# 128-column weight loads, and value mixing of two batches at a time from a channel-major copy, in an attention and SwiGLU kernel

## The chip, the core and the metric

The kernel runs on one core of a Trainium2 chip. Times are device microseconds of one execution. Ratios are always taken between fast runs of the same call on the same chip, because the median of the kernel before moved between 309.9 and 312.1 us from call to call. A run more than 1.5% above the fastest of its kernel counts as slow and is left out of the ratios.

The engines are named as the profile names them: PE is TensorE (matmuls), PEld its weight loads, DVE VectorE, ACT ScalarE, POOL GpSimd. An eviction copies a result from a PSUM tile, where the kernel's matmuls put it, to SBUF. The head is the first part of a run, until the attention of batch 0 is done (about 52 us in the kernel before).

## The reference, cut to what matters

Batch 4, 8 heads, 768 positions, head width 64, 8 blocks of 96 positions. A Sinkhorn iteration makes an 8 x 8 mixing matrix P for each head. Keys and values are mixed block by block with P, then attention runs inside each block, and a SwiGLU feed-forward follows over all 3072 tokens.

```python
k_sorted = einsum('bhij,bhjcd->bhicd', P, k_b)
v_sorted = einsum('bhij,bhjcd->bhicd', P, v_b)
scores = scale * matmul(q_b, k_sorted^T)          # 96 x 96 in each block
attn = exp(scores) / sum(exp(scores))
x = matmul(attn, v_sorted)                        # 96 x 64 in each block
out = (silu(x @ w_gate) * (x @ w_val)) @ w_out    # 512 -> 1536 -> 512
```

## The kernel before

A batch has 64 rows of (head, block); two batches share one SBUF tile of values. The parts that the change touches:

```python
# values of one batch: 64 partitions, [96 positions (padded to 128), 64 channels]
v_tiles[b] = vnp.tile([128, 128, D], BF16, ...)       # odd b uses the tile of b - 1

def drain(dst, src):          # evictions from PSUM: DVE and ACT by turns
    ...

def emit_v(b):                # value mixing: 64 matmuls for a batch
    for db in range(D // 8):
        tp = psum.tile([128, 8, H * NB], FP32, name="tv", tag="att")
        for ld in range(8):
            nc.tensor.matmul(tp[:, ld, :], lhsT=nat[lo:lo + R, :, db * 8 + ld],
                             rhs=vmix[b][lo:lo + R].rearrange("p a b -> p (a b)"), ...)
        drain(dst[:, :, ts(db, 8)], tp[0:C].transpose([0, 2, 1]))

def emit_qk(kqt, half, g):    # scores: 96-column weight loads
        nc.tensor.matmul(pss[two][:, i4, :], lhsT=kqt[lo:lo + D, 0, g, i, :],
                         rhs=kqt[lo:lo + D, 1, g, i, :], ...)

def emit_av(vt, half, g, es, xt):   # attention-value: 96-column weight loads
        nc.tensor.matmul(av[:, two, i4, :], lhsT=es[two][:, i4, :],
                         rhs=vt[:, 2 * g + two, half * 4 + i4, :], ...)
...
emit_att(0)
for b in range(B):
    if b + 1 < B:
        emit_att(b + 1)       # k/q mixing, scores, value mixing, attention-value
    emit_gv(b, 0); emit_gv(b, 1)      # gate and value projections
    emit_out(b, 0); emit_out(b, 1)
```

In `emit_v` the weights (`lhsT`) are one channel of the values: 64 rows, 128 columns, with 64 elements (128 bytes) from one column to the next. Attention of batch b+1 and feed-forward of batch b overlap; the order of the instructions comes from a scheduler and is fixed when the kernel is built.

The softmax here doesn't subtract the row's maximum and nothing guards it: scores larger than these inputs give would overflow.

## Time and profile before

| | before |
|---|---|
| median of 3 runs | 312.47 us (311.78 to 312.83) |
| PE busy | 92% of the span |
| value mixing (tv) on the chain that ended last | 8% of the span |
| PE at half clock, as recorded | 61 us of 311 |

The first lines are from the page of the kernel before. "PE" gives busy time, share of the span and instructions; "PEclk" gives the granted TensorE clock in tenths for 40 equal slices of 7.8 us; the last line is the chain that ended last, by line.

```profile
PE 285.2 (92%) x2736; PEld 176.8 (57%) x2736; DVE 174.1 (56%) x372; ACT 122.5 (39%) x246; POOL 24.7 (8%) x46
PEclk9996558875999999758999999859999999999999
...
PE v_ps L279 22%; PE g_ps L270 22%; PE o_ps L290 20%; PE tv L203 8%; PE av_ps L229 6%; PE tkq L189 4%; PE x_ps L239 3%; DVE st L235 1%; DVE kqt_1830 L176 0%; DVE kqt_2853 L176 0%; DVE colred L130 0%; DVE p_sb L132 0%; DVE p_sb L129 0%; DVE rowred L128 0%; DVE r_sb L233 0%
```

PE is the bottleneck, and its clock falls to half in five places. The groups by line and shape of the kernel before show the weight loads (busy us, then mean ns of one, then idle time before):

```profile
L203 PEld LDWEIGHTS <-v_233 64*128 64x128 bf16 x128 | 12.1, 212 | 2.6 <-issue 2.6
L239 PEld LDWEIGHTS <-st 96*128 96x128 bf16 x128 | 8.4, 105 | 9.6 <-DVE st L235 7.8 <-issue 0.7
...
L203 PE MATMUL tv<-vmix_125,v_233 64*128 64x64 bf16 x64 | 6.5, 270 | 0.0
...
L176 DVE CAST vt_2076<-tv 96x512 bf16<-96x512 f32 x4 | 2.8, 702 | 3.8 <-PE tv L203 3.8
```

The load with the 128-byte step takes 212 ns on record, the contiguous load of the same 128 columns 105 ns. A matmul's record (270 ns) is not the pace, since the next matmul starts long before it ends. The pace I took from the trace as the difference between the starts of successive matmuls of one group; "apart" below always means that, as a median. For mixing it is 90 ns. The timeline of PE in the mixing of batch 2 shows the same: 16 matmuls take about 1.6 us.

```profile
126.27 0.91 PE L203 MATMUL tv<-vmix_125,v_233 64*128 64x64 bf16 x8
127.11 0.34 PE L279 MATMUL v_ps<-xt_0_1024,wv_sb 128*128 128x384 bf16 x1
127.38 1.63 PE L203 MATMUL tv<-vmix_125,v_233 64*128 64x64 bf16 x16
...
129.38 1.63 PE L203 MATMUL tv<-vmix_125,v_233 64*128 64x64 bf16 x16
```

And these are three of the half-clock stretches in the table by stretches (stretch, its length, busy time of PE, PEld, DVE, ACT, POOL, then the clock, the DMA share and GB/s):

```profile
66.50:76.70 10.20, 10.20 (x75) 6.96 (x74) 3.87 (x8) 4.12 (x7) 0.00 (x0) 0.50 0.87 180
127.90:141.60 13.70, 13.70 (x103) 9.29 (x102) 5.76 (x12) 5.01 (x9) 0.00 (x0) 0.50 0.00 1
199.60:209.90 10.30, 10.30 (x73) 6.83 (x73) 4.03 (x7) 3.90 (x8) 0.00 (x0) 0.50 0.00 0
```

PE counts as busy for the whole of each stretch, and still its clock is halved.

One caution for every trace here: the clock record begins only with the first rise to full clock (18.7 us in this trace), and PEclk counts the time before it as full. It was half. Most k/q-mixing matmuls (64 columns) have records of 241 ns before 18.7 us, as in the recorded stretches at half clock (241 ns), and of 196 ns at recorded full clock. So PE worked at half clock for another 5 us here (13.6 to 18.7 us), 67 us in all. Totals of half clock below are of the recorded stretches unless the text says otherwise.

### The profile page before, as it was taken

What the parts mean: (1) busy time and instruction counts of PE and PEld (TensorE: products, weight loads), DVE (VectorE), ACT (ScalarE), POOL (GpSimd) and SP (SyncE); (2) the same over time, 40 slices, a digit from 0 to 9 for tenths busy, and PEclk for the clock granted to TensorE, in tenths of its full rate; (3) what the DMA queues carried; (4) which work ended last, traced back from release to release, by engine and by line L of the source; (5) the groups of instructions that cost most, each with busy time, mean ns of one, the idle gap of its engine ahead of it and who ended that gap; (6) DMA issues with size and microseconds to landing.
All of it is one profiled execution on the core that took longest, in us unless ns stands there. A gap on an engine that the chain in (4) does not pass through costs nothing.

```text
span 311.2 us, 6473 instructions
## 1 busy us (share of the span) xinstructions
PE 285.2 (92%) x2736; PEld 176.8 (57%) x2736; DVE 174.1 (56%) x372; ACT 122.5 (39%) x246; POOL 24.7 (8%) x46
## 2 busy tenths in 40 slices
PE   0269899699999999999999999999999999999994
PEld 0259566566766546766665546766655545555541
DVE  7753457543998405347988504438988403888500
ACT  2064353444654225445533224536533223333221
POOL 8554410100000000000000000000000000000000
PEclk9996558875999999758999999859999999999999
DMA  6999999996000021000000022000000022000022
GB/s 108 182 146 196 212 209 214 219 212 138 2 0 2 35 103 70 2 0 2 0 3 0 2 101 103 2 0 3 2 0 0 26 100 80 2 0 1 2 101 101
DMA packets 13388, 20.86 MB, mean 67 GB/s; under 512 B 1072, under 2 KB 8752, under 8 KB 13104
## 3 DMA queue, kind: packets, MB, share of 16 engines
q0 software_dynamic: 9856, 14.16, 27.4%
q1 hardware_dynamic: 3504, 6.30, 5.4%
q8 instruction: 21, 0.34, 0.4%
q14 instruction: 7, 0.06, 0.1%
HBM read 28.32 MB, written 6.29 MB: 111 GB/s over the span
## 4 chain that ended last, share of the span: by engine, by line
PE 88%; DVE 6%; issue 2%; ACT 2%; ACTq 0%
PE v_ps L279 22%; PE g_ps L270 22%; PE o_ps L290 20%; PE tv L203 8%; PE av_ps L229 6%; PE tkq L189 4%; PE x_ps L239 3%; DVE st L235 1%; DVE kqt_1830 L176 0%; DVE kqt_2853 L176 0%; DVE colred L130 0%; DVE p_sb L132 0%; DVE p_sb L129 0%; DVE rowred L128 0%; DVE r_sb L233 0%
## 5 line engine op out<-in xcount | busy, mean ns | idle before, releaser
L273 ACT ACTIVATE th_sb<-g_ps 128x384 bf16<-128x384 f32 x96 | 47.1, 490 | 71.6 <-PE g_ps L270 71.3
L275 DVE SCALAR_TENSOR_TENSOR gs_sb<-th_sb,g_ps 128x384 bf16<-128x384 bf16 x96 | 52.9, 551 | 31.0 <-ACT th_sb L273 25.0
L279 PEld LDWEIGHTS <-wv_sb 128*128 128x128 bf16 x384 | 37.8, 100 | 25.5 <-issue 2.2
L270 PEld LDWEIGHTS <-wg_sb 128*128 128x128 bf16 x384 | 37.5, 102 | 24.8 <-issue 4.1
L293 ACT COPY o_sb<-o_ps 128x512 f32<-128x512 f32 x24 | 14.0, 585 | 51.3 <-PE o_ps L290 51.3
L235 DVE TENSOR_TENSOR st<-av_ps,r_sb 96x512 bf16<-96x512 f32 x32 | 21.9, 683 | 0.7
L233 DVE RECIPROCAL r_sb<-av_ps 96x8 f32<-96x8 f32 x32 | 6.4, 201 | 18.0 <-PE av_ps L229 17.8
L270 PE MATMUL g_ps<-xt_0_459,wg_sb 128*128 128x384 bf16 x48 | 15.2, 406 | 0.0
L279 PE MATMUL v_ps<-xt_0_459,wv_sb 128*128 128x384 bf16 x48 | 15.0, 404 | 0.0
L239 PEld LDWEIGHTS <-st 96*128 96x128 bf16 x128 | 8.4, 105 | 9.6 <-DVE st L235 7.8
L203 PEld LDWEIGHTS <-v_233 64*128 64x128 bf16 x128 | 12.1, 212 | 2.6 <-issue 2.6
L239 PE MATMUL x_ps<-ident,st 96*128 96x96 bf16 x128 | 12.0, 222 | 1.3 <-DVE st L235 1.0
L142 PE MATMUL w_ps<-selb,lmix 32*64 32x4 bf16 x16 | 0.6, 191 | 13.6 <-DVE lmix L136 13.6
L203 PEld LDWEIGHTS <-v_135 64*128 64x128 bf16 x128 | 11.8, 213 | 1.3 <-issue 1.3
L176 DVE CAST kqt_1830<-tkq 128x512 bf16<-128x512 f32 x6 | 4.0, 690 | 15.3 <-PE tkq L189 15.3
L176 DVE CAST kqt_2853<-tkq 128x512 bf16<-128x512 f32 x6 | 4.0, 689 | 15.3 <-PE tkq L189 15.3
L270 PE MATMUL g_ps<-xt_0_1024,wg_sb 128*128 128x384 bf16 x48 | 12.1, 362 | 0.0
L279 PE MATMUL v_ps<-xt_0_1024,wv_sb 128*128 128x384 bf16 x48 | 12.0, 359 | 0.0
L270 PE MATMUL g_ps<-xt_0_2047,wg_sb 128*128 128x384 bf16 x48 | 11.9, 358 | 0.0
L279 PE MATMUL v_ps<-xt_0_2047,wv_sb 128*128 128x384 bf16 x48 | 11.4, 345 | 0.0
L270 PE MATMUL g_ps<-xt_1_636,wg_sb 128*128 128x384 bf16 x48 | 10.1, 325 | 0.0
L279 PE MATMUL v_ps<-xt_1_636,wv_sb 128*128 128x384 bf16 x48 | 9.9, 326 | 0.0
(388 smaller groups left out, 500.0 us busy)
## 6 DMA issues: line engine op xcount, KB each, us to landing
out_dram<-o_sb SPq DMA_DIRECT2D x24, 256.0 KB, 2.0
wg_sb<-in_moe_w_gate_dram POOLq DMA_DIRECT2D x6, 256.0 KB, 10.8
wv_sb<-in_moe_w_val_dram POOLq DMA_DIRECT2D x6, 256.0 KB, 10.7
wo_sb<-in_moe_w_out_dram POOLq DMA_DIRECT2D x1, 1536.0 KB, 21.5
v_233<-in_v_dram POOLq DMA_DIRECT2D x2, 768.0 KB, 21.2
kq_99<-in_k_dram POOLq DMA_DIRECT2D x4, 192.0 KB, 5.6
kq_99<-in_q_dram POOLq DMA_DIRECT2D x4, 192.0 KB, 6.3
v_135<-in_v_dram POOLq DMA_DIRECT2D x4, 192.0 KB, 10.2
```

The costliest lines, as they stand in the source:

```text
L176: nc.vector.tensor_copy(dst, src)
L189: nc.tensor.matmul(tp[two * D:(two + 1) * D, lc, :], lhsT=nat[:, cb * 8 + lc, :], rhs=rm[:, two, :], start=True, stop=True)
L203: nc.tensor.matmul(tp[:, ld, :], lhsT=nat[lo:lo + R, :, db * 8 + ld], rhs=vmix[b][lo:lo + R].rearrange("p a b -> p (a b)"), start=True, st ...
L229: nc.tensor.matmul(av[:, two, i4, :], lhsT=es[two][:, i4, :], rhs=vt[:, 2 * g + two, half * 4 + i4, :], start=True, stop=True)
L235: nc.vector.tensor_tensor(st.rearrange("p i two d -> p two i d"), av[:, :, :, 0:D], r_sb.to_broadcast([C, 2, 4, D]), op=ALU.mult)
L239: nc.tensor.transpose(x_ps[:, i4, :], st[:, i4].rearrange("p a b -> p (a b)"), ident[0:C, 0:C])
L270: nc.tensor.matmul(g_ps, lhsT=wg_sb[:, kc, ts(m, 128)], rhs=xt[:, kc, :], start=(kc == 0), stop=(kc == NKC - 1))
L273: nc.scalar.activation(th_sb, g_ps, AF.Tanh, scale=0.5)
L275: nc.vector.scalar_tensor_tensor(gs_sb, th_sb, 1.0, g_ps, op0=ALU.add, op1=ALU.mult)
L279: nc.tensor.matmul(v_ps, lhsT=wv_sb[:, kc, ts(m, 128)], rhs=xt[:, kc, :], start=(kc == 0), stop=(kc == NKC - 1))
L290: nc.tensor.matmul(o_ps, lhsT=h_w[:, m, ts(t3, 128)], rhs=wo_sb[:, m, :], start=(m == 0), stop=(m == NFC - 1))
L293: nc.scalar.copy(o_sb, o_ps)
```

## The change

It has three parts. Scores and attention-value load 128 weight columns where 96 are used; the surplus output rows are ignored. Values are mixed for two batches at once: 128 rows, 128 streamed columns, half as many matmuls, and no mixing in batches 1 and 3. The weights of the mixing come from a copy in which the columns of one channel lie side by side; VectorE makes it for batches 0 and 1, GpSimd for 2 and 3.

```diff
-    epool = ctx.enter_context(tc.tile_pool(name="epool", bufs=8))
+    epool = ctx.enter_context(tc.tile_pool(name="epool", bufs=1))
+    e_ring = [epool.tile([C, 4 * C + 32], BF16, name=f"er{n}") for n in range(8)]
...
-    vmix = [const.tile([128, H, NB], BF16, name=f"vmix{b}") for b in range(B)]
+    vmix = [const.tile([128, 2, H, NB], BF16, name=f"vmix{p}") for p in range(B // 2)]
+    vch = const.tile([128, D, 128], BF16, name="vch")
+    nc.vector.memset(vch[:, :, C:], 0.0)
...
-    load_v(0, 4)
+    load_v(0, 2)              # both batches of the pair
...
+    def emit_vch(pair):
+        nat = v_tiles[pair]
+        for s in range(4):
+            cs = slice(s * (C // 4), (s + 1) * (C // 4))
+            eng = nc.gpsimd if pair else nc.vector
+            eng.tensor_copy(vch[:, :, cs], nat[:, cs, :].transpose([0, 2, 1]))
...
-        for db in range(D // 8):
-            tp = psum.tile([128, 8, H * NB], FP32, name="tv", tag="att")
-            for ld in range(8):
-                nc.tensor.matmul(tp[:, ld, :], lhsT=nat[lo:lo + R, :, db * 8 + ld],
-                                 rhs=vmix[b][lo:lo + R].rearrange("p a b -> p (a b)"),
+        emit_vch(pair)
+        for db in range(D // 4):
+            tp = psum.tile([128, 4, 2 * H * NB], FP32, name="tv", tag="att")
+            for ld in range(4):
+                nc.tensor.matmul(tp[:, ld, :], lhsT=vch[:, db * 4 + ld, :], rhs=mix,
...
-                nc.tensor.matmul(pss[two][:, i4, :], lhsT=kqt[lo:lo + D, 0, g, i, :],
+                nc.tensor.matmul(pss[two][:, i4, :], lhsT=flat[lo:lo + D, at:at + 128],
...
-                nc.tensor.matmul(av[:, two, i4, :], lhsT=es[two][:, i4, :],
+                nc.tensor.matmul(av[:, two, i4, :], lhsT=es[two][:, i4 * C:i4 * C + 128],
```

Left out: buffer counts (`natp` 3 to 2, `vnp` 2 to 1), how the loads of the values are cut, slices of the outputs to 96 rows, and the bookkeeping of pairs.

More of the change, by code (lines that the diff above doesn't have):

```diff
@@ L54 @@
     const = ctx.enter_context(tc.tile_pool(name="const", bufs=1))
-    natp = ctx.enter_context(tc.tile_pool(name="natp", bufs=3))
-    vnp = ctx.enter_context(tc.tile_pool(name="vnp", bufs=2))
+    natp = ctx.enter_context(tc.tile_pool(name="natp", bufs=2))
+    vnp = ctx.enter_context(tc.tile_pool(name="vnp", bufs=1))
     kqp = ctx.enter_context(tc.tile_pool(name="kqp", bufs=2))
     vtp = ctx.enter_context(tc.tile_pool(name="vtp", bufs=2))
-    epool = ctx.enter_context(tc.tile_pool(name="epool", bufs=8))
+    epool = ctx.enter_context(tc.tile_pool(name="epool", bufs=1))
     ssp = ctx.enter_context(tc.tile_pool(name="ssp", bufs=3))
@@ L69 @@
     nc.sync.dma_start(out=p_sb, in_=sn)
+    e_ring = [epool.tile([C, 4 * C + 32], BF16, name=f"er{n}") for n in range(8)]
+    ecount = [0]
+    for e in e_ring:
+        nc.vector.memset(e[:, 4 * C:], 0.0)
     kq_tiles, v_tiles = {}, {}
@@ L78, in load_kq, with load_v @@
         kq_tiles[b] = t
-    def load_v(b, parts):
-        if b % 2 == 0:
-            v_tiles[b] = vnp.tile([128, 128, D], BF16, name=f"v{b}", tag="vn")
-            nc.vector.memset(v_tiles[b][:, C:, :], 0.0)
-        else:
-            v_tiles[b] = v_tiles[b - 1]
-        lo = (b % 2) * R
-        n = R // parts
+    def load_v(pair, parts):
+        t = vnp.tile([128, C, D], BF16, name=f"v{pair}", tag="vn")
+        step = C // parts
         for s in range(parts):
-            nc.gpsimd.dma_start(out=v_tiles[b][lo + s * n:lo + (s + 1) * n, 0:C],
-                                in_=v_nat[b, s * n:(s + 1) * n])
+            for u in range(2):
+                nc.gpsimd.dma_start(out=t[u * R:(u + 1) * R, s * step:(s + 1) * step],
+                                    in_=v_nat[2 * pair + u, :, s * step:(s + 1) * step])
+        v_tiles[pair] = t
     wg_sb = wpool.tile([128, NKC, DF], BF16)
@@ L114 @@
     rmix = [const.tile([128, 2, 2, H2, NB], BF16, name=f"rmix{b}") for b in range(B)]
-    vmix = [const.tile([128, H, NB], BF16, name=f"vmix{b}") for b in range(B)]
+    vmix = [const.tile([128, 2, H, NB], BF16, name=f"vmix{p}") for p in range(B // 2)]
+    vch = const.tile([128, D, 128], BF16, name="vch")
+    nc.vector.memset(vch[:, :, C:], 0.0)
+    for p in range(B // 2):
+        nc.vector.memset(vmix[p], 0.0)
     idq = ident[R:2 * R, R:2 * R].rearrange("p (g two j) -> p two g j", two=2, j=NB)
@@ L153 @@
         nc.vector.tensor_tensor(
-            vmix[b][lo:lo + R],
+            vmix[b // 2][lo:lo + R, b % 2],
             mask[lo:lo + R].unsqueeze(2).to_broadcast([R, H, NB]),
@@ L164 @@
     load_kq(1, [0, 48, 96])
-    load_v(1, 1)
     nc.gpsimd.dma_start(out=wo_sb, in_=wo_dram)
     load_kq(2, [0, 48, 96])
-    load_v(2, 1)
+    load_v(1, 2)
     load_kq(3, [0, 48, 96])
-    load_v(3, 1)
     tog = [0]
@@ L193, in emit_kq @@
         return dst.rearrange("p (a g i) c -> p a g i c", a=2, g=H2)
-    def emit_v(b):
-        nat = v_tiles[b]
-        lo = (b % 2) * R
-        dst = vtp.tile([C, H * NB, D + 1], BF16, name=f"vt{b}", tag="vt")
-        nc.vector.memset(dst[:, :, D:D + 1], 1.0)
-        for db in range(D // 8):
-            tp = psum.tile([128, 8, H * NB], FP32, name="tv", tag="att")
-            for ld in range(8):
-                nc.tensor.matmul(tp[:, ld, :], lhsT=nat[lo:lo + R, :, db * 8 + ld],
-                                 rhs=vmix[b][lo:lo + R].rearrange("p a b -> p (a b)"),
-                                 start=True, stop=True)
-            drain(dst[:, :, ts(db, 8)], tp[0:C].transpose([0, 2, 1]))
-        return dst.rearrange("p (h i) d -> p h i d", h=H)
+    def emit_vch(pair):
[4 more added lines that the diff above has]
+            eng.tensor_copy(vch[:, :, cs], nat[:, cs, :].transpose([0, 2, 1]))
@@ new lines, in emit_v @@
+    def emit_v(pair):
+        emit_vch(pair)
+        dst = vtp.tile([C, 2 * H * NB, D + 1], BF16, name=f"vt{pair}", tag="vt")
+        nc.vector.memset(dst[:, :, D:D + 1], 1.0)
+        mix = vmix[pair].rearrange("p u a b -> p (u a b)")
+        for db in range(D // 4):
+            tp = psum.tile([128, 4, 2 * H * NB], FP32, name="tv", tag="att")
+            for ld in range(4):
+                nc.tensor.matmul(tp[:, ld, :], lhsT=vch[:, db * 4 + ld, :],
+                                 rhs=mix, start=True, stop=True)
+            drain(dst[:, :, ts(db, 4)], tp[0:C].transpose([0, 2, 1]))
+        return dst.rearrange("p (u h i) d -> p u h i d", u=2, h=H)
@@ L209, in emit_qk @@
+    vts = {}
     def emit_qk(kqt, half, g):
         es = []
-        pss = [psum.tile([C, 4, C], FP32, name=f"qk{two}", tag="att") for two in range(2)]
+        pss = [psum.tile([128, 4, C], FP32, name=f"qk{two}", tag="att") for two in range(2)]
+        flat = kqt.rearrange("p a g i c -> p (a g i c)")
         for i4 in range(4):
             i = half * 4 + i4
+            at = (g * NB + i) * C
             for two in range(2):
                 lo = two * D
-                nc.tensor.matmul(pss[two][:, i4, :], lhsT=kqt[lo:lo + D, 0, g, i, :],
+                nc.tensor.matmul(pss[two][:, i4, :], lhsT=flat[lo:lo + D, at:at + 128],
@@ L217, in emit_qk @@
                                  rhs=kqt[lo:lo + D, 1, g, i, :], start=True, stop=True)
         for two in range(2):
-            e = epool.tile([C, 4, C], BF16, name=f"e{two}", tag="e")
-            nc.scalar.activation(e, pss[two], AF.Exp, scale=scale)
+            e = e_ring[ecount[0] % len(e_ring)]
+            ecount[0] += 1
+            nc.scalar.activation(e[:, 0:4 * C], pss[two][0:C].rearrange("p a c -> p (a c)"),
+                                 AF.Exp, scale=scale)
             es.append(e)
@@ L224, in emit_av @@
     def emit_av(vt, half, g, es, xt):
-        av_ps = psum.tile([C, 2, 512], FP32, name="av_ps", tag="av", bufs=1)
+        av_ps = psum.tile([128, 2, 512], FP32, name="av_ps", tag="av", bufs=1)
         av = av_ps[:, :, 0:4 * (D + 1)].rearrange("p two (i e) -> p two i e", e=D + 1)
@@ L232, in emit_av @@
         r_sb = ssp.tile([C, 2, 4, 1], FP32, name="r_sb", tag="r")
-        nc.vector.reciprocal(r_sb, av[:, :, :, D:D + 1])
+        nc.vector.reciprocal(r_sb, av[0:C, :, :, D:D + 1])
         st = ssp.tile([C, 4, 2, D], BF16, name="st", tag="st")
-        nc.vector.tensor_tensor(st.rearrange("p i two d -> p two i d"), av[:, :, :, 0:D],
+        nc.vector.tensor_tensor(st.rearrange("p i two d -> p two i d"), av[0:C, :, :, 0:D],
                                 r_sb.to_broadcast([C, 2, 4, D]), op=ALU.mult)
@@ L254, in emit_att @@
             if vt is None and len(pend) == 2:
-                vt = emit_v(b)
+                if b % 2 == 0:
+                    vts[b // 2] = emit_v(b // 2)
+                vt = vts[b // 2][:, b % 2]
             if len(pend) > 2:
```

## The prediction

> **What bounds the kernel now.** TensorE. The page gives PE 92% busy, and the chain of waits is 88% PE; in the table by stretches PE is above 96% busy everywhere from 75 to 292 us. PE time saved there is saved in full. The head differs: until about 24 us PE waits for the Sinkhorn chain and for k, q and v to land.
>
> **Where the change works.**
> - Value mixing (tv, L203): 256 matmuls, 64 per batch, 8% of the chain. From start to start they take 90 ns (median), at full and at half clock alike, although they stream only 64 columns. The weight load with its 128-byte step sets that pace: its records average 212 ns, those of contiguous 128-column loads 98 to 105 ns.
> - Attention-value (av, L229), 96-column loads: 45 ns apart at full clock, 80 ns at half clock, for 65 streamed columns. The transposes (L239), 128-column loads, are 42 ns apart for 96. [...]
> - Scores (L216): a pair takes about 41 ns for 96 columns, already set by the stream. I expect almost nothing there.
> - Clock: the PEclk row and the timeline show half clock for about 61 us: 25.5-49.4, 59.7-63.1, 66.5-76.7, 127.9-141.6, 199.6-209.9. Four of these five begin in or right beside value mixing. At half clock 69 gate/value matmuls start about 320 ns apart in place of 162: about 11 us, and about 5 us more on the small ones.
>
> **Costs, estimated from these.**
> - tv becomes 128 matmuls of 128 streamed columns, two batches at once. Interpolated between 42 ns (96 columns) and 162 ns (384), 55 ns each: 7 us in place of 25. Evictions stay 32 of 0.70 us on two engines, so a pair needs at least 5.7 us for its 16 tiles and is eviction-bound unless feed-forward matmuls fill in. Batches 1 and 3 lose their 6.5 us each, batch 2 about 3, batch 0 nothing: -16 us.
> - av: 256 x 10 to 15 ns: -3 us.
> - Clock: batches 1 and 3 have no mixing phase, batch 2 a dense one. Most of the half-clock stretches after 63 us should go: -6 us.
> - Head: mixing of batch 0 now needs both batches' values (0.8 MB more at about 0.2 MB/us: up to 4 us[...]) and four strided VectorE copies of 1536 elements ([...], two of them after the last landing). Mixing starts at 25 to 29 us in place of 24: +3 us. Dense mixing may bring the clock back before 49 us: -2 us.
> - Pair 1's copies run on GpSimd long before they are needed: 0.
>
> Sum: 312.5 - 16 - 3 - 6 + 1 = 288 us, range 279 to 299. Chances: faster 0.94, same 0.05, slower 0.01.
>
> **What would show it.** tv: 128 matmuls, 55 to 60 ns apart at full clock, weight-load records near 100 ns. av 30 to 38 ns apart. Scores unchanged. No half clock near 200 us, less near 130. First tv at 25 to 29 us. Batches 1 and 3 go from scores straight to av. PE still above 90%.
>
> **What would make it wrong.** The copies cost 3 us or more each and hold the head; mixing of batch 2 stalls on evictions unfilled, so the clock falls there as before; half clock follows the many small attention matmuls, not the mixing, and stays; or a new instruction order moves feed-forward work out of the attention stages.

The forecast's sum came to 288 us: -16, -3, -6, and +1, which is +3 and -2 us for the head. The -3 us are the author's estimate from 45 ns for 65 streamed columns with a 96-column load and 42 ns for 96 with a 128-column load. The 0.2 MB/us are the GB/s row of the page before: 146 to 212 GB/s from 7.8 to 47 us.

## The result

| | before | after |
|---|---|---|
| median | 312.12 us (4 runs) | 287.39 us (4 runs, 286.65 to 287.90) |
| ratio of fast runs | | 0.921 (95% interval 0.917 to 0.925) |
| PE at half clock in the profiled run, as recorded | 61 us | 17 us |
| the same with the time before the first clock record | 67 us | 32 us |

A ratio is the mean time of one kernel's fast runs over that of the other's of the same rounds, so it is not quite the ratio of the medians quoted. The forecast was 288 us.

The page of the kernel after:

```profile
PE 257.2 (90%) x2600; PEld 152.7 (53%) x2608; DVE 178.9 (63%) x383; ACT 121.7 (43%) x246; POOL 39.1 (14%) x51
PEclk9999955979999999999999999999999999999999
...
PE v_ps L297 22%; PE g_ps L288 22%; PE o_ps L308 22%; PE av_ps L245 4%; PE qk L230 4%; PE tkq L193 3%; PE x_ps L255 3%; PE tv L214 3%; DVE kqt L180 2%; DVE vch L204 1%; DVE st L251 1%; ACT vt L182 1%; DVE vt L180 1%; ACT th_sb L291 1%; DVE colred L136 0%
```

The mixing's share of the chain fell from 8% to 3%, and after the first third the clock row holds nines only. Its nines in the first 28.8 us are not a full clock: there is no record before 28.8 us, k/q-mixing matmuls take 241 ns there, and value-mixing matmuls are 107 ns apart until then and 55 ns after. New on the chain is `DVE vch` (the new copies), and `DVE kqt` (evictions of mixed keys and queries) grew: 0.5% for each of the two tiles listed before, 2% now. The instructions that touch the copy in the kernel after (count, then minimum, median and maximum ns of one, first and last start, form):

```profile
L214 PEld LDWEIGHTS <-vch x128: 95/97/152, 25.6 to 123.9; 128*128 128x128 bf16 x128
L214 PE MATMUL tv<-vmix,vch x128: 216/219/314, 25.6 to 123.9; 128*128 128x128 bf16 x128
L204 DVE COPY vch<-v x4: 1465/1494/1509, 16.6 to 23.9; 128x1536 bf16<-128x1536 bf16 x4
L204 POOL COPY vch<-v x4: 2871/2877/2889, 64.3 to 72.7; 128x1536 bf16<-128x1536 bf16 x4
```

Mixing matmuls are now 56 ns apart (median of all). In the mixing of batch 2, from 116.3 to 124.1 us, groups of four or eight stand between feed-forward matmuls, and the clock stays full. First the timeline of PE, then the stretch in the table by stretches:

```profile
116.36 0.39 PE L214 MATMUL tv<-vmix,vch 128*128 128x128 bf16 x4
116.59 0.33 PE L297 MATMUL v_ps<-xt,wv_sb 128*128 128x384 bf16 x1
116.75 0.39 PE L214 MATMUL tv<-vmix,vch 128*128 128x128 bf16 x4
...
118.23 0.65 PE L288 MATMUL g_ps<-xt,wg_sb 128*128 128x384 bf16 x3
118.89 0.61 PE L214 MATMUL tv<-vmix,vch 128*128 128x128 bf16 x8
```

```profile
116.30:124.20 7.90, 7.56 (x84) 5.43 (x83) 7.02 (x12) 6.85 (x12) 0.00 (x0) 1.00 0.00 0
```

DVE and ACT are 89% and 87% busy there: this stretch has moved close to its evictions, which take longer in the new form (page of the kernel after; 702 ns before, 785 ns now):

```profile
L180 DVE CAST vt<-tv 96x512 bf16<-96x512 f32 x16 | 12.2, 785 | 2.7 <-PE tv L214 2.5
```

If each PE instruction is charged with the time from its start to the start of the next matmul, the two traces can be compared in full. The differences add up to 25.8 us, while the two spans differ by 25.3 us:

| charged to | before, us | after, us |
|---|---|---|
| value mixing | 24.5 | 12.0 |
| gate and value projections | 141.3 | 134.4 |
| attention-value | 15.9 | 10.9 |
| scores | 16.6 | 12.3 |
| k/q mixing | 22.9 | 26.4 |
| transposes | 9.0 | 8.4 |
| output projection | 62.1 | 62.1 |

The change touches neither the gate nor the value projections, yet they lost 6.9 us: that is the clock. In the recorded half-clock stretches 69 of their matmuls ran before and 26 after, and 43 times the difference between 320 and 162 ns is 6.8 us. Eight attention-value matmuls at full clock, first in the kernel before (two groups of four), then after:

```profile
143.64 0.37 PE L229 MATMUL av_ps<-vt_2076,e_2168 96*96 96x65 bf16 x4
143.84 0.34 PE L229 MATMUL av_ps<-vt_2076,e_2170 96*96 96x65 bf16 x4
131.44 0.43 PE L245 MATMUL av_ps<-vt,er 96*128 96x65 bf16 x8
```

The k/q mixing grew by 3.5 us: that is the head, where VectorE now does the copies between the evictions that this mixing waits for. VectorE in the head of the kernel after (start, us, line, form, count):

```profile
18.06 1.29 DVE L180 CAST kqt<-tkq 128x512 bf16<-128x512 f32 x2
19.26 1.51 DVE L204 COPY vch<-v 128x1536 bf16<-128x1536 bf16 x1
20.69 1.28 DVE L180 CAST kqt<-tkq 128x512 bf16<-128x512 f32 x2
21.88 1.48 DVE L204 COPY vch<-v 128x1536 bf16<-128x1536 bf16 x1
23.28 0.68 DVE L180 CAST kqt<-tkq 128x512 bf16<-128x512 f32 x1
```

The first scores came at 24.11 us, against 21.01 us before. In the timelines of PE (after, then before), they now wait for an eviction on VectorE:

```profile
24.11 0.80 PE L230 MATMUL qk<-kqt 64*128 64x96 bf16 x12 [1.45 <-DVE kqt L180]
21.01 0.24 PE L216 MATMUL qk_460<-kqt_242 64*96 64x96 bf16 x1 [0.68 <-ACT kqt_242 L178]
```

### The profile page after: what moved, and what is told of

It reads as the page before. It is cut to its first block, busy times and chain, and to the rows that moved or that the text cites. A ratio compares the mean times of both kernels' runs of the same rounds, so it can differ in the third digit from the quotient of the medians.

```text
span 285.9 us, 6221 instructions
## 1 busy us (share of the span) xinstructions
PE 257.2 (90%) x2600; PEld 152.7 (53%) x2608; DVE 178.9 (63%) x383; ACT 121.7 (43%) x246; POOL 39.1 (14%) x51
## 4 chain that ended last, share of the span: by engine, by line
PE 82%; DVE 11%; ACT 3%; issue 2%; ACTq 0%
PE v_ps L297 22%; PE g_ps L288 22%; PE o_ps L308 22%; PE av_ps L245 4%; PE qk L230 4%; PE tkq L193 3%; PE x_ps L255 3%; PE tv L214 3%; DVE kqt L180 2%; DVE vch L204 1%; DVE st L251 1%; ACT vt L182 1%; DVE vt L180 1%; ACT th_sb L291 1%; DVE colred L136 0%
## 5 line engine op out<-in xcount | busy, mean ns | idle before, releaser
L288 PE MATMUL g_ps<-xt,wg_sb 128*128 128x384 bf16 x384 | 84.8, 331 | 0.2 <-DVE h L299 0.2
L297 PE MATMUL v_ps<-xt,wv_sb 128*128 128x384 bf16 x384 | 82.1, 331 | 0.0
L308 PE MATMUL o_ps<-wo_sb,h 128*128 128x512 bf16 x280 | 62.4, 379 | 0.4
L299 DVE SCALAR_TENSOR_TENSOR h<-v_ps,gs_sb 128x384 bf16<-128x384 f32 x96 | 53.1, 553 | 9.0 <-PE v_ps L297 0.8
L297 PEld LDWEIGHTS <-wv_sb 128*128 128x128 bf16 x384 | 36.8, 98 | 24.5 <-issue 0.8
L308 PEld LDWEIGHTS <-h 128*128 128x128 bf16 x288 | 28.2, 98 | 33.6
L180 DVE CAST kqt<-tkq 128x512 bf16<-128x512 f32 x24 | 15.9, 688 | 33.9 <-PE tkq L193 33.9
L311 ACT COPY o_sb<-o_ps 128x512 f32<-128x512 f32 x24 | 14.1, 586 | 51.4 <-PE o_ps L308 51.4
L235 ACT ACTIVATE er<-qk 96x384 bf16<-96x384 f32 x64 | 27.1, 487 | 12.2 <-PE qk L230 12.2
L193 PE MATMUL tkq<-rmix,kq 128*64 128x64 bf16 x768 | 20.3, 212 | 5.5 <-issue 2.5
L193 PEld LDWEIGHTS <-kq 128*64 128x64 bf16 x768 | 17.7, 126 | 8.9 <-issue 7.9
L182 ACT CAST kqt<-tkq 128x512 bf16<-128x512 f32 x24 | 14.1, 586 | 15.7 <-PE tkq L193 15.6
L245 PE MATMUL av_ps<-vt,er 96*128 96x65 bf16 x256 | 14.9, 202 | 0.2 <-ACT vt L182 0.2
L182 ACT CAST vt<-tv 96x512 bf16<-96x512 f32 x16 | 12.5, 787 | 2.1 <-PE tv L214 1.8
## 6 DMA issues: line engine op xcount, KB each, us to landing
kq<-in_q_dram POOLq DMA_DIRECT2D x6, 384.0 KB, 12.1
wg_sb<-in_moe_w_gate_dram POOLq DMA_DIRECT2D x6, 256.0 KB, 11.8
```

Source lines behind the costliest of these rows:

```text
L180: nc.vector.tensor_copy(dst, src)
L182: nc.scalar.copy(dst, src)
L193: nc.tensor.matmul(tp[two * D:(two + 1) * D, lc, :], lhsT=nat[:, cb * 8 + lc, :], rhs=rm[:, two, :], start=True, stop=True)
L235: nc.scalar.activation(e[:, 0:4 * C], pss[two][0:C].rearrange("p a c -> p (a c)"), AF.Exp, scale=scale)
L245: nc.tensor.matmul(av[:, two, i4, :], lhsT=es[two][:, i4 * C:i4 * C + 128], rhs=vt[:, 2 * g + two, half * 4 + i4, :], start=True, stop=True)
L288: nc.tensor.matmul(g_ps, lhsT=wg_sb[:, kc, ts(m, 128)], rhs=xt[:, kc, :], start=(kc == 0), stop=(kc == NKC - 1))
```

## The experiments

The prediction hit the time, so the question was whether it hit for its reasons: which part gave how much, what the copy is worth, and what sets the clock. Twelve kernels ran; all were correct. Where two of them are compared by their ratios, both ratios are to the kernel before.

### 1. Only the 128-column loads of scores and attention-value

The kernel before with these edits of the change and no other:

```diff
-                nc.tensor.matmul(pss[two][:, i4, :], lhsT=kqt[lo:lo + D, 0, g, i, :],
+                nc.tensor.matmul(pss[two][:, i4, :], lhsT=flat[lo:lo + D, at:at + 128],
-                nc.tensor.matmul(av[:, two, i4, :], lhsT=es[two][:, i4, :],
+                nc.tensor.matmul(av[:, two, i4, :], lhsT=es[two][:, i4 * C:i4 * C + 128],
```

> The kernel before with only the 128-column weight loads of scores and attention-value; value mixing as before. Theory (loads give PE time only): av goes from 45 to about 33 ns apart and a unit of scores from 0.31 to 0.27 us, over 32 units 4 to 5 us, so about 307 us (304 to 309); mixing still 90 ns apart and half clock still 50 us or more. Rival (half clock follows the many small attention matmuls, so the fast loads lift it): half clock under 35 us and about 300 us.

Measured: 305.20 us, ratio 0.982 (0.974 to 0.991). Attention-value matmuls went from 45 to 33 ns apart at full clock and from 80 to 54 ns at half clock. Half clock stayed at 51 us. So the loads are worth about 5.6 us between the means (310.95 and 305.33 us; 3 to 8 us by the interval), and most of the half clock stays.

### 2. Only the mixing

The kernel after with these two edits reverted.

```diff
-                nc.tensor.matmul(pss[two][:, i4, :], lhsT=flat[lo:lo + D, at:at + 128],
+                nc.tensor.matmul(pss[two][:, i4, :], lhsT=kqt[lo:lo + D, 0, g, i, :],
-                nc.tensor.matmul(av[:, two, i4, :], lhsT=es[two][:, i4 * C:i4 * C + 128],
+                nc.tensor.matmul(av[:, two, i4, :], lhsT=es[two][:, i4, :],
```

> The kernel after with 96-column loads for scores and attention-value; value mixing as after. Theory: 5 us slower than after, about 292 us (290 to 295), av back at 45 ns; half clock under 30 us, since the mixing is what brought it down. Rival: half clock back at 40 us or more and 298 us or more.

Measured: 291.66 us, ratio 0.938 (0.930 to 0.945); half clock 17 us, as in the kernel after. About 19.3 us of the gain belong to the new mixing (310.95 less 291.65 us, means). Parts 1 and 2 add up to 24.9 us; the whole change gave 24.4 us (means). So, within intervals of about 2.5 us to either side, the two halves of the change add.

### 3. Pairs, but no copy

```diff
-        t = vnp.tile([128, C, D], BF16, name=f"v{pair}", tag="vn")
+        t = vnp.tile([128, 128, D], BF16, name=f"v{pair}", tag="vn")
+        nc.vector.memset(t[:, C:, :], 0.0)
...
-        emit_vch(pair)
+        nat = v_tiles[pair]
...
-                nc.tensor.matmul(tp[:, ld, :], lhsT=vch[:, db * 4 + ld, :],
+                nc.tensor.matmul(tp[:, ld, :], lhsT=nat[:, :, db * 4 + ld],
```

> The kernel after, but pairs are mixed straight from the loaded tile with its 128-byte step; no channel-major copy. Theory (the step of the load sets the pace; pairing halves the loads): 128 mixing matmuls 90 ns apart, 11.5 us in all against 25 before and 7 to 12 after; scores of batch 0 begin at 21 us and not 24, since VectorE copies no values. So near after: 284 to 290 us. Rival (the contiguous copy is what pays): 293 us or more, and half clock back near the mixing of batch 2.

Measured: 284.89 us, ratio 0.917 (0.910 to 0.923). The mixing matmuls were 91 ns apart, with 128 streamed columns as with 64 before (90 ns); without the step they are 56 ns apart in the kernel after. Yet the run was no slower than the kernel after. The first scores came at 21.00 us, because VectorE had only evictions to do in the head of this run:

```profile
15.90 1.39 DVE L179 CAST kqt<-tkq 128x512 bf16<-128x512 f32 x2
17.46 1.51 DVE L179 CAST kqt<-tkq 128x512 bf16<-128x512 f32 x2 [0.16 <-PE tkq L192]
19.14 1.35 DVE L179 CAST kqt<-tkq 128x512 bf16<-128x512 f32 x2 [0.17 <-PE tkq L192]
```

PE time charged to mixing was 14.1 us against 12.0: the copy buys 2 us of PE, and the scores come 3 us later with it. The evictions of mixed values took 0.84 us here on VectorE (median), against 0.78 us in the kernel after; this is not explained. Pairing alone is enough. Runs 11 and 12 compare the two on one chip.

The clock rises later with the copy, too. In the five traces with copies on VectorE (the kernel after and runs 2, 4, 7 and 12) the clock first rose at 28.8 to 44.9 us, in the nine without at 17.9 to 21.1 us. How much of the copy's price is this and how much the later scores, no run separates.

### 4. The copy, but no pairs

```diff
-        for db in range(D // 4): ...  lhsT=vch[:, db * 4 + ld, :], rhs=mix     # 128 streamed columns
+        for u in range(2):
+            for db in range(D // 8): ...  lhsT=vch[lo:lo + R, db * 8 + ld, :],
+                                          rhs=mix                               # 64 rows, 64 columns
```

> The kernel after with the channel-major copy, but each batch mixed by itself: 256 matmuls of 64 rows and 64 streamed columns. Theory (pace is the larger of load and stream): 33 to 40 ns apart, 9 to 10 us of PE in all, evictions back at 0.70 us; time as after within 2 us (286 to 290). Rival (half clock comes from mixing that uses only 64 rows and 64 columns): half clock again beside mixing of batch 2, and 291 us or more.

Measured: 289.13 us, ratio 0.928 (0.921 to 0.936). The mixing took 12.1 us in all, evictions 0.69 us on VectorE. The matmuls of batches 0 and 1 were 53 ns apart, those of batches 2 and 3 29 ns, as 16 of each show:

```profile
30.82 1.03 PE L217 MATMUL tv<-vmix,vch 64*128 64x64 bf16 x16
118.12 0.64 PE L217 MATMUL tv<-vmix,vch 64*128 64x64 bf16 x16
```

The first are at half clock: the clock record of this trace begins at 44.9 us. There was no half clock beside the mixing of batch 2. In all there were 10 us on record, and 42 us with the time before the record. So the rival was wrong for batch 2, while in the head the clock stayed at half throughout this mixing of 64 rows; in the kernel after it rose at 28.8 us, within the mixing of 128 rows. Against the kernel after (0.921) the difference in time is not separable in these runs. So the step can be made harmless in either of two ways: half as many loads, or loads without a step. The change does both and needs one.

### 5. The mixing before, streamed twice as wide

This run tests what brings the clock down. The 64 columns are streamed twice; the next matmul overwrites the surplus.

```diff
-                nc.tensor.matmul(tp[:, ld, :], lhsT=nat[lo:lo + R, :, db * 8 + ld],
-                                 rhs=vmix[b][lo:lo + R].rearrange("p a b -> p (a b)"),
+                n = 2 if ld < 7 else 1
+                mix = vmix[b][lo:lo + R].rearrange("p a b -> p (a b)")
+                nc.tensor.matmul(tp[:, ld:ld + n, :], lhsT=nat[lo:lo + R, :, db * 8 + ld],
+                                 rhs=mix.unsqueeze(1).to_broadcast([R, n, H * NB]),
```

> The kernel before; in value mixing 7 of 8 matmuls stream their 64 columns twice (128 columns; the second 64 are overwritten by the next matmul). Still 256 strided loads of 64 rows. Theory (half clock comes where the array streams for too small a share of the time: 64 columns are 27 ns at full clock out of 90 ns, 128 columns 55 ns out of 90): mixing keeps 90 ns and 24 to 25 us of PE, but the half-clock stretches beside mixing of batches 1 to 3 go, half clock falls from 61 to under 30 us and the time to 301 to 305 us. Rival (rows in use, or the small attention matmuls, decide): half clock stays at 50 us or more and the time at 310 us or more.

The 27 ns are an estimate from the traces: matmuls of 384 columns are 162 ns apart at full clock, a sixth of which is 27 ns. The 55 ns are the pace of mixing with 128 columns in the kernel after.

Measured: 308.74 us, ratio 0.993 (0.986 to 0.999). The theory fell. Half clock still began in each mixing, though each stretch was now 6.8 us long and not 10.2 or 13.7 us; 48 us in all. (The rival's 50 us and 310 us were not quite reached either.) In this run's table by stretches, mixing of batch 2 and the stretch that follows:

```profile
123.20:129.30 6.10, 6.10 (x68) 6.10 (x68) 2.89 (x4) 2.73 (x6) 0.00 (x0) 0.94 0.01 3
128.60:135.40 6.80, 6.80 (x53) 4.65 (x52) 3.41 (x7) 2.78 (x6) 0.00 (x0) 0.50 0.00 0
```

The share of time in which columns stream is not the whole of it.

### 6. A mixture: pair 0 without the copy, pair 1 with it

```diff
-            eng = nc.gpsimd if pair else nc.vector
-            eng.tensor_copy(vch[:, :, cs], nat[:, cs, :].transpose([0, 2, 1]))
+            nc.gpsimd.tensor_copy(vch[:, :, cs], nat[:, cs, :].transpose([0, 2, 1]))
...
-                nc.tensor.matmul(tp[:, ld, :], lhsT=vch[:, db * 4 + ld, :],
+                nc.tensor.matmul(tp[:, ld, :], lhsT=vch[:, db * 4 + ld, :] if pair else nat[:, :, db * 4 + ld],
```

> The kernel after, but pair 0 mixed straight from the loaded tile (no VectorE copies), pair 1 from the GpSimd copy; one xt buffer less for space. Theory (the copies cost in the head only; the contiguous load pays in batch 2 only): first scores at 21 us and not 24, mixing of batch 2 at 56 ns, 282 to 285 us, 1 to 2 us below the run with no copy at all. Rival (batch 2 is bound by evictions, so the copy gives nothing there): 285 us, as the run with no copy.

Measured: 284.26 us, ratio 0.915 (0.910 to 0.919), not separable from run 3. The first scores came at 21.83 us. Its first matmul came 0.8 us late (14.39 us): two memsets of 0.91 us now stand on VectorE before the Sinkhorn chain. Run 9 takes that up.

### 7. The copies of pair 0 made twice

```diff
-            eng.tensor_copy(vch[:, :, cs], nat[:, cs, :].transpose([0, 2, 1]))
+            for _ in range(1 if pair else 2):
+                eng.tensor_copy(vch[:, :, cs], nat[:, cs, :].transpose([0, 2, 1]))
```

> The kernel after with each of the four VectorE copies of pair 0 made twice. Theory (the copies stand in VectorE's order between the k/q evictions that the scores of batch 0 wait for): 4 more copies of 1.49 us, first scores 4 to 6 us later and 4 to 6 us more in all, 291 to 294 us. Rival (they hide behind the landing of v and k/q): under 2 us more.

Measured: 291.26 us, ratio 0.939 (0.934 to 0.944), against 0.921 for the kernel after. The size fits the theory, the place does not. The scores came at 24.47 us, hardly later; the scheduler put the extra copies behind the evictions, five in a row, and the first mixing matmul came at 31.2 us and not 25.6. VectorE in the head of this run:

```profile
23.62 0.70 DVE L180 CAST kqt<-tkq 128x512 bf16<-128x512 f32 x1
24.22 6.93 DVE L205 COPY vch<-v 128x1536 bf16<-128x1536 bf16 x5
31.86 1.64 DVE L180 CAST vt<-tv 96x512 bf16<-96x512 f32 x2 [0.70 <-PE tv L215]
```

So these extra 6.0 us of copies were paid nearly in full (0.939 less 0.921 of the time before, about 5.6 us), although they stand behind the evictions. The first four copies, also 6.0 us, cost less: 1 to 3 us by runs 3, 11 and 12.

### 8. Pairs without the copy, streamed half as wide

Run 3 with two matmuls of 64 streamed columns for each channel: 256 loads with the step, 128 rows.

```diff
-                nc.tensor.matmul(tp[:, ld, :], lhsT=nat[:, :, db * 4 + ld], rhs=mix, ...)
+                for u in range(2):
+                    us = slice(u * H * NB, (u + 1) * H * NB)
+                    nc.tensor.matmul(tp[:, ld, us], lhsT=nat[:, :, db * 4 + ld], rhs=mix[:, us], ...)
```

> The run with pairs and no copy, but each value column is mixed by two matmuls of 64 streamed columns: 256 strided loads of 128 rows. Theory (share of streaming decides the clock): half clock comes back in or just after mixing of batch 2, and about 10 us of PE are added (128 more loads at 90 ns, partly hidden by evictions in the head): 294 to 299 us. Rival (using all 128 rows is enough for the clock): as slow by the loads, 292 to 296 us, but no half clock after 60 us.

Measured: 295.44 us, ratio 0.954 (0.946 to 0.962). 90 ns apart with 64 streamed columns, as in the kernel before, and yet no half clock came after 69.3 us while PE worked. One stretch did come after 60 us, from 62.4 to 69.3 us, in the attention of batch 1, where no values are mixed. The table by stretches for its mixing of batch 2:

```profile
118.00:131.30 13.30, 13.30 (x145) 12.94 (x145) 8.29 (x12) 7.55 (x12) 0.00 (x0) 1.00 0.01 1
```

For the mixing of batch 2 the rival won: the clock there was 1.00 with 128 rows, and 0.50 after the mixing with 64 rows in run 5. In these runs the rows count too. Its "no half clock after 60 us" was too strong.

### A count from the ten traces, and its test

In the clock records the clock is 0.5 or 1, and the stretches at half clock last 3.41 us or a whole multiple of it, up to 27.31 us (8 times, run 5), unless the run ends first. So I cut each trace into windows of 3.41 us, in phase with its own clock changes, and summed for each window the streaming time of the matmuls that start in it, weighted by the share of 128 rows and of 128 weight columns that they use; no matmul in the traces uses more of either. A streamed column counts as 0.42 ns at full clock and as 0.83 ns at half clock. The traces show these rates: 512 columns are 216 ns apart at full clock, 384 columns 162 ns at full and 320 ns at half clock. The share is a count from the forms of the instructions. What decides the clock, and on which windows, is not recorded; the windows are my estimate from the length of the stretches.

In all 14 traces (before, after and twelve runs), from 36 us on, there are 944 windows at full clock. Half clock followed 19 of them, and their share was 0.17 to 0.32. It did not follow the other 925, and the lowest share among those was 0.36. Neither of the simpler counts separates the two: by streaming time alone, windows fell at up to 0.58 and stayed at 0.40; with rows but without weight columns, they fell at up to 0.58 and stayed at 0.38; with weight columns but without rows, at up to 0.55 and at 0.39. To come back to full clock took more: the lowest window before a rise had 0.67, but others stayed at half clock with up to 0.80, so this side has no clean limit. Before 36 us these limits do not hold cleanly (windows fell at up to 0.37, and stayed at down to 0.30), and what happens in the head stays open.

The limits were found in the ten traces up to run 8. In the four made after it (runs 9 to 12), one window fell, at 0.18, and the lowest of the 274 that stayed had 0.39.

### 9. The mixture with a late memset

```diff
-    nc.vector.memset(vch[:, :, C:], 0.0)
...
     def emit_vch(pair):
+        nc.gpsimd.memset(vch[:, :, C:], 0.0)
```

> The hybrid (pair 0 straight from the loaded tile, pair 1 from the GpSimd copy), with the pad of the copy zeroed on GpSimd just before the copies. In the hybrid that zeroing (0.91 us) stood on VectorE ahead of the Sinkhorn chain and the first matmul came at 14.39 us, not 13.56. Theory: first matmul back at 13.6 us, 283 to 284 us, the lowest of all. Rival (the head waits for the k and q loads, not for the Sinkhorn chain): no change, 284 to 285 us.

Measured: 283.27 us, ratio 0.909 (0.903 to 0.915). First matmul at 13.56 us. Its median is the lowest of all, but its interval overlaps that of run 11 (0.913), and its ratio leaves out two runs of 284.3 and 284.4 us as slow, against one fast run of 279.62 us. So the mixture cannot be said to beat the simpler form.

### 10. The mixing before, over the full array

The kernel before with all its 256 loads with the step, 64 for each batch, as run 5; but the streamed operand has 128 rows, zeros for the other batch. The values of batch 1 are loaded right after those of batch 0. PE does nothing less than before. The cut is shown against run 5; left out are the zeroing of `vmix` and the moved load.

```diff
-                nc.tensor.matmul(tp[:, ld:ld + n, :], lhsT=nat[lo:lo + R, :, db * 8 + ld],
-                                 rhs=mix.unsqueeze(1).to_broadcast([R, n, H * NB]),
+                nc.tensor.matmul(tp[:, ld:ld + n, :], lhsT=nat[:, :, db * 8 + ld],
+                                 rhs=mix.unsqueeze(1).to_broadcast([128, n, H * NB]),
```

> The kernel before with its 256 strided loads at 90 ns, 64 per batch, but mixing uses all 128 rows (zeros in the streamed operand for the other batch) and 128 columns: the same loads, no time saved on PE. Counting for each window of 3.4 us the share of rows x columns x streaming time, all falls to half clock seen in the ten traces so far after 35 us came from windows at 0.32 or less, and every window that kept full clock was at 0.34 or more. Here mixing should be near 0.5. Theory: no half clock begins in the mixing of batches 1, 2 and 3 (near 65, 125 and 193 us), and the time falls by 4 to 7 us from the clock alone, to 304 to 308 us (later values in the head may cost 1 to 2 us of it). Rival (mixing as such, its waits or its interleaving, brings the fall): half clock there as in the run with the wide stream, 308 us or more.

The share near 0.5 is an estimate: 120 streamed columns in the mean, at 0.42 ns each, make 50 of the 90 ns.

Measured: 300.06 us, ratio 0.965 (0.959 to 0.971). The mixing took its 90 ns as before, and no half clock began in the mixing of batches 1, 2 or 3. The stretch from 59.5 to 62.9 us stayed; it begins in the k/q mixing of batch 1, after a wait of 2.4 us. The table by stretches for batch 2, mixing and the 13.7 us after it:

```profile
122.40:128.30 5.90, 5.90 (x68) 5.86 (x68) 2.92 (x4) 2.86 (x6) 0.00 (x0) 1.00 0.01 3
128.30:142.00 13.70, 13.70 (x164) 9.23 (x164) 11.60 (x26) 9.17 (x21) 0.00 (x0) 1.00 0.00 1
```

In the 13.7 us at half clock before, the table counted 103 matmuls; here 164. The means differ by 10.8 us (310.41 and 299.60): more than the 4 to 7 us that I had expected from the clock. Run 5 differs from this one in the rows and in when the values of batch 1 are loaded; it had 0.993. The moved load acts in the head, but of the 11.8 us between the two profiled spans 8.0 us lie after the first output projection begins (103.9 us before, 100.1 us here). This shows the clock's worth by itself, with no load and no matmul saved.

### 11 and 12. No copy and the kernel after, once more on one chip

Run 11 is the kernel of run 3, run 12 the kernel after.

> The run with pairs and no copy again, for a comparison on one chip with the kernel after and the hybrid: 284 to 286 us, 2 to 3 us below the kernel after if the copies of pair 0 are a net cost; equal to it if the first difference was chance.

> The kernel after again, on one chip with the two before it: 286.5 to 288.5 us.

Measured: 283.86 us, ratio 0.913 (0.908 to 0.918), and 286.12 us, ratio 0.923 (0.917 to 0.928); both just below what was expected. The kernel without the copy was lower both times: the first time by 0.005 of the time before, the second by 0.010. The intervals overlap a little, so the size of 1 to 3 us is not exact, but nothing in these runs speaks for the copy on VectorE.

## Why the prediction was right, point by point

The time was right, 288 forecast and 287.4 measured. So were the direction of the large terms and most of the marks it named: 55 ns for mixing at full clock (55 to 60), load records of 97 ns (near 100), 33 ns for attention-value (30 to 38), first mixing at 25.6 us (25 to 29), no half clock near 200 or 130 us. PE was 90% busy, not above it. But that the sum came within 1 us was luck: errors of its terms cancelled.

- **Mixing, forecast -16 us: -12.5 us of PE time.** The failing step was "batch 0 nothing" and evictions of 0.70 us. In the new form an eviction takes 0.785 us, and in the head the mixing of the pair took 7.2 us (25.6 to 32.8) against 5.9 us for batch 0 alone. Until 28.8 us four matmuls at half clock took 0.43 us, a little more than the 0.39 us per tile of evictions on two engines; after that four took 0.22 us, and the evictions bound it. What the copy added was not worth its price: pairs alone (run 3) did as well.
- **Clock, forecast -6 and -2 us: about -10.8 us by run 10**, where it is measured alone. After 63 us the recorded 34 us at half clock went entirely. The -2 us for the head did not show: from the first matmul to 49 us PE spent 29 us at half clock before and 29 us after. The cause was half named. Mixing did bring the clock down, but "dense" was not the point: run 8 kept the clock with 64 columns at 90 ns, and run 5 lost it with 128. Rows, weight columns and streaming time together separate the windows from 36 us on (0.32 at most and 0.36 at least).
- **128-column loads, forecast -3 us and "almost nothing" for scores: -5.6 us together (run 1).** The attention-value part alone lost 5.0 us of PE time in the kernel after, some of it at half clock. Scores were not indifferent: in the traces, a unit of 8 score matmuls and the switch behind it took 0.28 us at full clock, against 0.31 us before. The pair's pace of 41 ns was read from the middle of a unit; from the first pair to the second it went from 80 ns to 53 ns.
- **Head, forecast +3 and -2 us: about +3 us for the scores, of another cause.** I had charged a later landing of values and copies after it. In the trace the copies stand between the k/q evictions on VectorE and hold the scores (24.1 and not 21.0 us); without copies they are at 21.0 us (run 3). The clock's later rise with the copies (28.8 us) is not separated from this.

These measured terms sum to about -26 us, against 24.4 us measured. They overlap in part, so the sum is a check and no proof.

Two comparisons of weight loads were a good base. Attention-value matmuls with 96-column loads were 45 ns apart at full and 80 ns at half clock, with 128-column loads 33 and 54 ns in the same place. Loads with a step of 64 elements (128 bytes) gave 90 ns from load to load, at full and at half clock alike; contiguous columns gave, at full clock, 55 ns with 128 streamed columns, and 29 ns with 64 (run 4).

## What to carry to other kernels

Use all 128 rows and weight columns in small matmuls where that adds no instruction: here small matmuls on part of the rows and columns cost nearly as much through the clock (10.8 us, run 10) as the change saved of their own time (12.5 us), and a window can lose the clock while the profile calls PE busy (3.37 of the 3.41 us before 127.9 us in the kernel before). The clock record began later than the kernel did (at 18.7 us before, at 28.8 us after): check it against the pace of the matmuls. When loads are slow, first use each load for more (pair batches) before paying another engine to rearrange the data (0.913 without the copy in run 11, 0.923 with it in run 12); check where that rearrangement stands in the other engine's order. When a forecast hits, take its terms apart all the same.
